# The first batch of an attention and mixer kernel as one explicit order of steps, with four MLP accumulations begun among the last mixer pieces

## The chip, the cores and the metric

The kernel runs on one core of one Trainium2 chip. The metric is the device time of one execution in microseconds (us). TensorE (PE) multiplies and writes PSUM; VectorE (DVE), ScalarE (ACT) and GpSimd (POOL) do the rest; SyncE (SP) and POOL issue DMAs. Each engine executes its own instructions in the order of the program and waits for others through semaphores.

## The reference

Eight sequences of 448 tokens, 12 heads of 64. Attention with normalised queries and keys, then a mixer that adds a low-rank mix over the tokens, then an MLP of 768 to 3072 to 768:

```python
q_n, k_n = rmsnorm(q, g_q), rmsnorm(k, g_k)
attn = softmax(q_n @ k_n.T / sqrt(64))
x = (attn @ v) with the heads side by side        # 8 x 448 x 768
h = x.transpose(0, 2, 1) @ U @ V                  # rank 32, over the tokens
u = x + h.transpose(0, 2, 1)
out = u + relu(u @ w_ch1) @ w_ch2
```

## The kernel before, in words

Heads are taken in groups of four (24 groups, three to a batch), and in pairs of heads (six to a batch). For a group, q and k are loaded (`load`, SP), squared (`squares`), summed (`sums`, DVE), turned into 1/rms (`roots`, two small ACT steps), scaled (`scale`, mostly POOL), transposed on PE (`turn`) and copied out of PSUM (`take_q`, `take_k`). `values` (POOL) casts v. For a pair, `Sc` multiplies keys and queries in four steps r = 0 to 3 (the first three write 128x896, the last 128x448) and ACT takes the exponential of each; `V` multiplies the exponentials with the values in two halves, and DVE divides by the sums into `x`.

For batch 0, `mix_t0` multiplies x with U, and `mix(dt)` makes one of six 128-row pieces of `uT`, the mixer's output, turned. An MLP accumulation `up(b, ht)` is six matmuls over the six pieces `dt` of `uT` with one of 24 column blocks of w1, then a relu; `down` multiplies with w2. w1 comes in four quarters and w2 in eight parts, cast on the way, all issued by POOL through `weights(n)`; the first quarter of w1 serves the accumulations 0 to 5.

The program order is fixed by hand (`tc.manual_schedule()`): what is called first stands first in the queue of its engine. Batch 0's attention is alone on the chip: the rows of `extra` say what is put behind which `Sc`, with `keep_busy` (dummy matmuls) where PE would stand still. Two MLP accumulations of batch 0 are begun early with `up_part` in one half of a score buffer each: three matmuls, one, and the last two in the MLP's list. From `first_done` on, a planner merges two lists: `att`, the attention of the next batches, and `mlp`, with estimated costs; `due(cm)` says how far attention should be, and `ready` holds a step back while ACT or DVE are behind PE. Group 3 belongs to batch 1; its squares and sums lie in the front, its scaling and turning at the head of the second part of `att`.

Score buffers (`ps_sc`) are two, of two PSUM banks each; all else in PSUM shares four buffers of one bank (`ps`).

Of the kernel before, what the change touches and what calls it, by code (L numbers as in the profile page):

```python
# [26 lines left out]
def kernel(  # L27
# [19 lines left out]
    P = 128  # L47
# [199 lines left out]
    for va, vl in zip(va_bufs, vl_bufs):  # L247
        nc.vector.memset(va[:, :, D:D1], 1.0)
        nc.vector.memset(vl, 0.0)
        for e in range(2):  # L250
            nc.vector.memset(vl[e * R:(e + 1) * R, :, e * D1 + D:(e + 1) * D1], 1.0)
# [9 lines left out]
    def prep_gains():  # L261
        m = gp[:, P:]
        nc.vector.tensor_reduce(m, gp[:, :D], AX, ALU.max, apply_absolute_value=True)
        nc.vector.tensor_scalar(m, m, -scal * D, EXP_ROOM, ALU.mult, ALU.add)
        nc.vector.tensor_scalar(m, m, 0.0, -EXP_SHIFT, ALU.min, ALU.max)
# [3 lines left out]
        return pg  # L269
# [42 lines left out]
    nc.gpsimd.memset(Vr[:, S:], 0.0)  # L312
# [15 lines left out]
    def fill_mixer():  # L328
        nc.gpsimd.memset(Uz, 0.0)

# [13 lines left out]
    def turn(gi, i):  # L344

        pt = pts[(gi, i)] = ps.tile([P, NT, 2, R], BF16, name="pt", tag="ps")
        pos = POS_ODD if i == 0 and groups[gi][0] % 2 else POS
        for j in range(NT):
            nc.tensor.transpose(pt[:, pos[j]].rearrange("p a r -> p (a r)"),  # L349
                                normed[gi][i][:, j].rearrange("p c d -> p (c d)"), ident)  # L350

    def take_q(gi, a, scalar=False):
# [6 lines left out]
        qk[(gi, a)] = [qT]  # L359

    def take_k(gi, a):
# [6 lines left out]
        qk[(gi, a)].append(kT)  # L368
# [29 lines left out]
    def Sc(b, pr, r):  # L398
# [9 lines left out]
        for i in range(n):  # L408
            d = slice(i * D, (i + 1) * D) if r < NJ else slice(0, P)
            nc.tensor.matmul(sc[:, i, :S], kT[d, keys], qT[d], start=True, stop=True)  # L410
        nc.scalar.activation(es[(b, pr)][:, 2 * r:2 * r + n, :], sc[:, :n, :S], AF.Exp, scale=scal, bias=bias)  # L411
        runs("pe", 0.25)
# [32 lines left out]
    def V(b, pr, half):  # L445
        at["pe"] = max(at["pe"], exp_done[(b, pr)])
# [5 lines left out]
        h0 = groups[gi][1] + first_h  # L452
        E = es[(b, pr)]
        pv = ps.tile([P, 2, 2, D1], FP32, name="pv", tag="ps")
        for i in range(2):
# [3 lines left out]
            for e in range(2):  # L459
                for j in range(NJ):  # L460
                    nc.tensor.matmul(pv[:, i, e, :], E[:, 2 * j + e, w:w + P],  # L461
                                     va[:, (first_h + step * e) * NJ + j, :], start=False, stop=(e == 1 and j == NJ - 1))
        r = headp.tile([P, 2, 2], FP32, name="r", tag="r")
# [4 lines left out]
            r.rearrange("p i e -> p i e ()").to_broadcast([P, 2, 2, D]), ALU.mult)  # L468
        runs("pe", 0.5)
        runs("dve", 0.6)  # L470

# [38 lines left out]
    def mix_t0(lo, hi, scalar=False):  # L510

        pt = ps.tile([P, 512], FP32, name="pu0", tag="ps")
        for j in range(NW):
            nc.tensor.matmul(pt[:, :hi - lo], Uz[:, j, :], xs[0][:, j, lo:hi], start=(j == 0), stop=(j == NW - 1))
        if scalar:
            nc.scalar.copy(tz[:, lo:hi], pt[:, :hi - lo])
        else:
            nc.vector.tensor_copy(tz[:, lo:hi], pt[:, :hi - lo])

    def mix(b, dt, scalar=False):  # L520
        off = 64 if b % 2 == 0 else 0
        ph = ps.tile([P, S], FP32, name="ph", tag="ps")
        xb = xs[b][:, :, dt * P:(dt + 1) * P]
# [4 lines left out]
        if scalar:  # L528
            nc.scalar.copy(uT[:, dt, off:off + S], ph)
        else:  # L530
            nc.vector.tensor_copy(uT[:, dt, off:off + S], ph)
# [36 lines left out]
    begun = {}  # L568

    def up_part(b, ht, lo, hi):  # L570
        off = 64 if b % 2 == 0 else 0
        if lo == 0:
            begun[(b, ht)] = ps_sc.tile([P, 2, 512], FP32, name="sc", tag="sc")[:, 0, :S]
        ph = begun[(b, ht)]
        for dt in range(lo, hi):
            nc.tensor.matmul(ph, w1b[:, dt, ht * P:(ht + 1) * P], uT[:, dt, off:off + S],
                             start=(dt == 0), stop=(dt == KD - 1))
        if hi == KD:
            nc.scalar.activation(hT[:, ht, off:off + S], ph, AF.Relu)
# [60 lines left out]
    def V2(i, half):  # L640
        return (0.55, V, (*pairs[i], half))

    pool = nc.gpsimd

    def scales(gi):
        return [(0, roots, (gi,)), (0, scale, (gi, 0, pool)), (0, scale, (gi, 1, pool))]

    def turns(gi):
        return [(0.4, turn, (gi, 0)), (0, take_q, (gi, 0)), (0, take_q, (gi, 1)), (0.4, turn, (gi, 1)), (0, take_k, (gi, 0))]

    extra = {
        (0, 0): [(0, keep_busy, (8,))],
        (0, 1): [(0, keep_busy, (8,))],
        (0, 2): scales(1) + [(0, squares, (2, 1, pool)), (0, keep_busy, (8,))],
        (0, 3): [(0, keep_busy, (8,))],
        (1, 0): [(0, keep_busy, (8,))],
        (1, 1): [V2(0, 0), (0, keep_busy, (6,))],
        (1, 2): [(0.4, turn, (1, 0)), (0, take_q, (1, 0)), (0, take_q, (1, 1)), (0, keep_busy, (8,))],
        (1, 3): [(0.4, turn, (1, 1)), (0, take_k, (1, 0)), V2(0, 1), (0, take_k, (1, 1)), (0, sums, (2, 1)),
                 (0, values, (1,)), (0, load, (4,)), (0, weights, (1,))],  # L660
        (2, 1): scales(2) + [(0, weights, (1,)), V2(1, 0)],
        (2, 2): [(0, keep_busy, (6,))],
        (2, 3): [V2(1, 1), (0, prep_u, ())],
        (3, 0): [(0, keep_busy, (6,))],
        (3, 1): [V2(2, 0)],
        (3, 2): turns(2),
        (3, 3): [V2(2, 1), (0, take_k, (2, 1)), (0, squares, (3, 0, pool)), (0, values, (2,)), (0, load, (5,)),
                 (0, weights, (1,)), (0, prep_v, ()), (0, squares, (3, 1, pool)), (0, weights, (1,))],
        (4, 0): [V2(3, 0)],
        (4, 1): [V2(3, 1), (0, sums, (3, 0))],  # L670
        (5, 0): [(0.9, mix_t0, (0, 512))],
        (5, 1): [V2(4, 0)],
        (5, 2): [V2(4, 1), (0.39, mix, (0, 0))],
        (5, 3): [(0.39, mix, (0, 1)), (0.2, mix_t0, (512, 640)), (0, weights, (2,))],
    }
    for i in range(NPAIR):
        for r in range(4):
            add_att(0.38, Sc, *pairs[i], r)
            att.extend(extra.get((i, r), []))
    att.extend([V2(5, 0), V2(5, 1), (0, sums, (3, 1)), (0.39, mix, (0, 2, True)), (0.39, mix, (0, 3, True)), (0.57, up_part, (0, 0, 0, 3)),  # L680
                (0.2, mix_t0, (640, dm)), (0.39, mix, (0, 4, True)), (0, roots, (3,)), (0.57, up_part, (0, 1, 0, 3)),
                (0.39, mix, (0, 5)), (0.19, up_part, (0, 0, 3, 4)), (0.19, up_part, (0, 1, 3, 4))])
    first_done = len(att)

    att.extend([*scales(3)[1:2], (0, scale, (3, 1, nc.vector)), (0, values, (3,)), (1.4, lambda: None, ()),
# [78 lines left out]
    done_at = {}  # L764
    for n, (c, f, a) in enumerate(att):
        if f is V and a[1] == NPAIR - 1 and a[2] == 1:
            done_at[a[0]] = n + 1 if a[0] > 0 else first_done
# [4 lines left out]
    for b in range(B):  # L772
        for ht in range(KH):
            mlp.append((0.38, up_part, (b, ht, 4, KD), b) if b == 0 and ht < 2 else (1.14, up, (b, ht), b))
            if b < ROWS_FROM and ht % 2 == 0 and ht < 4 * NW:
                mlp.append((0.17, mix_rows, (b, ht // 4, ht // 2 % 2), b))
# [21 lines left out]
    a_, b_ = PARTS  # L798
    squares_part(0, *a_)
    squares_part(0, *b_)  # L800
    sums_part(0, *a_)
    sums_part(0, *b_)
    squares_part(1, *a_)
    roots(0, 0, 1)
    squares_part(1, *b_)
    for part in PARTS:
        scale_part(0, *part, nc.gpsimd)
    for part in PARTS:
        sums_part(1, *part)
    roots(0, 1, 2)  # L810
    pg = prep_gains()
    keep_busy(10)
    for part in PARTS:
        scale_part(1, *part, nc.vector)
    nc.vector.tensor_copy(gg, pg)
    squares(1, 0)
    fill_mixer()
    squares(2, 0, nc.gpsimd,
            uT.rearrange("p k c -> p (k c)")[:, :4 * NT * D].bitcast(FP32).rearrange("p (j d) -> p j d", d=D))
    values(0)  # L820
    turn(0, 0)
    keep_busy(14)
    take_q(0, 0, True)
    take_q(0, 1, True)
    squares(1, 1)
    turn(0, 1)
    take_k(0, 0)
    sums(1, 0)
    sums(1, 1)
    take_k(0, 1)  # L830
    sums(2, 0)
    stage_tiles(3)
    load_u()
    load_v(2)
    load_qk(3, 0)
    load_qk(3, 1)
    load_v(3)

    ia = im = 0
# [109 lines left out]
```

## Time and profile before

| what | value |
|---|---|
| three runs | 577.03, 578.73, 578.82 us (median 578.73) |
| profiled execution | 577.21 us, span 575.3 us |
| granted TensorE clock | 0.999 |
| PE, ACT, POOL, DVE busy | 98%, 53%, 36%, 34% |
| DMA, mean | 119 GB/s over the span |
| first exponential starts | 11.61 us |
| last exponential of batch 0 ends | 35.10 us |
| last piece of `uT` of batch 0 is copied | 39.97 us |

The profile is of one execution; its times count from the start of the span, and the execution took 1.9 us more than the span. The first rows are of whole executions; the last three are rows of the timeline and say where the stage ends that the change is about.

### The profile page before, as it was taken

What the parts mean: (1) busy time and instruction counts of PE and PEld (TensorE: products, weight loads), DVE (VectorE), ACT (ScalarE), POOL (GpSimd) and SP (SyncE); (2) the same over time, 40 slices, a digit from 0 to 9 for tenths busy, and PEclk for the clock granted to TensorE, in tenths of its full rate; (3) what the DMA queues carried; (4) which work ended last, traced back from release to release, by engine and by line L of the source; (5) the groups of instructions that cost most, each with busy time, mean ns of one, the idle gap of its engine ahead of it and who ended that gap; (6) DMA issues with size and microseconds to landing.
All of it is one profiled execution on the core that took longest, in us unless ns stands there. A gap on an engine that the chain in (4) does not pass through costs nothing.

```text
span 575.3 us, 11525 instructions
## 1 busy us (share of the span) xinstructions
PE 565.6 (98%) x4723; PEld 326.0 (57%) x4724; DVE 194.2 (34%) x452; ACT 307.3 (53%) x510; POOL 205.3 (36%) x302
## 2 busy tenths in 40 slices
PE   8899999999999999999999999999999999999997
PEld 7655555555655555555556555555565555555565
DVE  6676655412343221631335330443033310410011
ACT  6867661677453876367654578367762444014300
POOL 4884683365423615324524423442531000000000
PEclk9999999999999999999999999999999999999999
DMA  9899999875436842597245835276204210320022
GB/s 244 161 242 241 245 230 216 147 166 118 126 66 168 176 115 35 97 212 180 33 128 106 188 100 131 58 184 152 35 14 97 57 28 1 61 70 1 1 55 56
DMA packets 104828, 68.19 MB, mean 119 GB/s; under 512 B 66632, under 2 KB 101704, under 8 KB 104776
## 3 DMA queue, kind: packets, MB, share of 16 engines
q1 hardware_dynamic: 95124, 57.83, 44.6%
q0 software_dynamic: 9408, 9.44, 9.8%
q8 instruction: 37, 0.61, 0.5%
q10 hardware_dynamic: 244, 0.20, 0.1%
q14 instruction: 15, 0.12, 0.1%
HBM read 52.20 MB, written 11.01 MB: 110 GB/s over the span
## 4 chain that ended last, share of the span: by engine, by line
PE 93%; DMA 2%; ACT 2%; POOL 1%; issue 1%; DVE 1%; SPq 0%; POOLq 0%; ACTq 0%
PE ph L558 38%; PE po L605 36%; PE pv L461 6%; PE sc L431 2%; PE pv L457 2%; PE sl L422 2%; PE sl L433 2%; PE po L592 1%; DMA qf<-in_q_dram 1%; PE sc L410 1%; DMA vf<-in_v_dram 1%; ACT E L411 1%; PE sc L496 1%; PE pt L349 1%; POOL kp L174 1%
## 5 line engine op out<-in xcount | busy, mean ns | idle before, releaser
L558 PE MATMUL ph<-uT,w1b 128*128 128x448 bf16 x1140 | 228.8, 352 | 0.0
L605 PE MATMUL po<-w2b,hT 128*128 128x384 bf16 x1296 | 223.8, 326 | 0.0
L605 PEld LDWEIGHTS <-hT 128*128 128x128 bf16 x1296 | 123.0, 98 | 79.0 <-issue 2.5
L558 PEld LDWEIGHTS <-w1b 128*128 128x128 bf16 x1140 | 108.2, 98 | 93.9 <-issue 1.1
L565 ACT ACTIVATE hT<-ph 128x448 bf16<-128x448 f32 x184 | 98.0, 553 | 118.7 <-PE ph L558 117.2
L381 POOL TENSOR_SCALAR qT<-qT,gg 128x448 bf16<-128x448 bf16 x36 | 50.4, 1403 | 87.4 <-DMA qT<-qn 79.6
L424 ACT ACTIVATE E<-sl,gg 128x448 bf16<-128x448 f32 x72 | 41.7, 634 | 69.8 <-PE sl L422 69.8
L464 DVE RECIPROCAL r<-pv 128x4 f32<-128x4 f32 x96 | 17.4, 181 | 167.4 <-PE pv L461 167.1
L193 POOL TENSOR_TENSOR qn<-qf,rs 128x384 bf16<-128x384 f32 x36 | 29.9, 830 | 120.8 <-ACT rs L170 114.6
L436 ACT ACTIVATE E<-sc,gg 128x896 bf16<-128x896 f32 x72 | 69.2, 1028 | 0.0
L615 DVE TENSOR_TENSOR ob<-po,x 128x384 f32<-128x384 f32 x46 | 25.6, 557 | 113.7 <-PE po L605 109.7
L461 PE MATMUL pv<-va,E 128*128 128x65 bf16 x1152 | 57.1, 194 | 0.0
L461 PEld LDWEIGHTS <-E 128*128 128x128 bf16 x1152 | 50.5, 98 | 6.2
L162 DVE TENSOR_REDUCE ssq<-sq 128x14 f32<-128x896 f32 x45 | 46.8, 1079 | 3.1 <-ACT sq L140 2.6
L457 PE MATMUL pv<-vl,E 128*128 128x130 bf16 x192 | 42.3, 220 | 0.3 <-ACT E L411 0.2
L465 DVE TENSOR_TENSOR x<-pv,r 128x256 bf16<-128x256 f32 x96 | 40.7, 424 | 3.3
L411 ACT ACTIVATE E<-sc,gg 128x896 bf16<-128x896 f32 (+1 forms) x42 | 37.5, 952 | 3.5 <-PE sc L410 3.4
L193 POOL TENSOR_TENSOR kp<-kf,rs 128x384 bf16<-128x384 f32 x36 | 29.8, 829 | 0.0
L503 DVE TENSOR_TENSOR x<-sc,x 128x384 bf16<-128x384 f32 x42 | 20.8, 551 | 15.7 <-PE sc L496 15.7
L169 ACT ACTIVATE rs<-ssq,eps 128x28 f32<-128x28 f32 (+1 forms) x25 | 7.9, 314 | 34.0 <-DVE ssq L162 31.3
L457 PEld LDWEIGHTS <-E 128*128 128x128 bf16 x192 | 18.7, 97 | 10.4 <-issue 2.7
L434 ACT ACTIVATE E<-sl,gg 128x448 bf16<-128x448 f32 x36 | 23.1, 642 | 0.0
(103 smaller groups left out, 364.5 us busy)
## 6 DMA issues: line engine op xcount, KB each, us to landing
qf<-in_q_dram SPq DMA_DIRECT2D x23, 448.0 KB, 3.9
kf<-in_k_dram SPq DMA_DIRECT2D x23, 448.0 KB, 5.0
vf<-in_v_dram SPq DMA_DIRECT2D x48, 192.0 KB, 5.6
out_dram<-ob SPq DMA_DIRECT2D x48, 192.0 KB, 2.7
w1b<-in_moe_w_ch_dram POOLq DMA_DIRECT2D x4, 1152.0 KB, 20.3
w2b<-in_moe_w_ch_dram POOLq DMA_DIRECT2D x8, 576.0 KB, 18.8
vf<-in_v_dram SPq DMA_DIRECT2D x48, 32.0 KB, 5.1
out_dram<-ob SPq DMA_DIRECT2D x13, 96.0 KB, 3.8
```

The lines of the kernel that those rows point to most:

```text
L162: nc.vector.tensor_reduce(ssqs[gi][:, i, :], sqs.pop((gi, i)), AX, ALU.add)
L193: nc.gpsimd.tensor_tensor(main.rearrange("p (t i) d -> p i t d", i=2), src[:, c, :2 * NJ].rearrange("p (i t) d -> p i t d", i=2), rs[:, c, ...
L381: nc.gpsimd.tensor_scalar(qT[:, a], qT[:, a], gg[:, 0:1], None, ALU.mult)
L411: nc.scalar.activation(es[(b, pr)][:, 2 * r:2 * r + n, :], sc[:, :n, :S], AF.Exp, scale=scal, bias=bias)
L424: nc.scalar.activation(E[:, 4 + i, :], ts[i], AF.Exp, scale=scal, bias=bias)
L436: nc.scalar.activation(E[:, 2 * r:2 * r + 2, :], tiles[r][:, :, :S], AF.Exp, scale=scal, bias=bias)
L457: nc.tensor.matmul(pv[:, i].rearrange("p e d -> p (e d)"), E[:, 2 * NJ, w:w + P], vl[:, lp, :], start=True, stop=False)
L461: nc.tensor.matmul(pv[:, i, e, :], E[:, 2 * j + e, w:w + P], va[:, (first_h + step * e) * NJ + j, :], start=False, stop=(e == 1 and j == N ...
L465: nc.vector.tensor_tensor(xs[b].rearrange("p i (h d) -> p i h d", d=D)[:, 2 * half:2 * half + 2, h0:h0 + step + 1:step, :], pv[:, :, :, :D ...
L558: nc.tensor.matmul(ph, w1b[:, dt, ht * P:(ht + 1) * P], uT[:, dt, off:off + S], start=(dt == 0), stop=(dt == KD - 1))
L565: nc.scalar.activation(hT[:, ht, off:off + S], ph, AF.Relu)
L605: nc.tensor.matmul(po, hT[:, ht, col:col + P], w2b[:, ht, half * HALF:(half + 1) * HALF], start=(ht == 0), stop=(ht == KH - 1))
```

## The change

Batch 0 is no longer given by `extra` and a prelude of calls, but by one string, `FRONT`, of steps in the order in which they are called. A step is `name.arguments:engine`. So every step of every engine has a place of its own: `S` and `E` are the two halves of `Sc` (matmuls, exponential), `V` and `N` those of `V` (matmuls, normalisation), `mt` and `mtc` those of `mix_t0` (now in four chunks of 256, 256, 128 and 128 columns instead of 512, 128 and 128), `mix` and `mc` those of `mix`. `sqp`, `smp`, `rt0`, `scp` are the parts of group 0; `sq`, `sm`, `rt`, `sc`, `tq`, `tk` are squares, sums, roots, scaling, `take_q`, `take_k`; `b` is `keep_busy`, `w` issues one quarter of w1, `u.ht.dt` is one matmul of an MLP accumulation. `:a`, `:v`, `:p` are ACT, DVE, POOL.

- Four MLP accumulations instead of two are begun, in the four banks of the two score buffers, and all 24 of their matmuls, with the relus, stand in the front. The MLP's list starts at accumulation 4.
- Squares: those of group 2's keys go from POOL to ACT; those of group 1's keys go ahead of those of its queries and ahead of `take_q` of group 0; group 0's go second part first. Group 3's stand behind the front on POOL.
- Sums, roots and scaling of group 3 go to the planner's part.
- Some fills go from DVE to POOL or back, two small steps on the gains from DVE to POOL, and their maximum ahead of group 0's sums.
- The quarters of w1 are issued at other places: the first behind `val.1`, where POOL no longer has the square of group 2's keys ahead of it.
- Group 0's turn has its pieces in another order, dummy matmuls go from 90 to 66 (without the 72 at the start), and `ready` lets a `Spair` go with ACT at most 0.6 behind PE, not 1.0.

```diff
-    for t, eng in zip(kT_bufs, (nc.vector, nc.gpsimd)):
-        eng.memset(t[D:P, :, SM:S], 0.0)
-        eng.memset(t[0:D, :, S:], 0.0)
+    for i in range(2):
+        fill_values(i, nc.vector)
+    fill_keys(0, nc.vector)
...
     def fill_mixer():
         nc.gpsimd.memset(Uz, 0.0)
+        fill_values(2, nc.gpsimd)
+        fill_keys(1, nc.gpsimd)
...
-    def up_part(b, ht, lo, hi):
...
+    AHEAD = 4
+    begun, dts = [], {}
+
+    def up_one(ht, dt):
+        if ht // 2 == len(begun):
+            begun.append(ps_sc.tile([P, 2, 512], FP32, name="sc", tag="sc"))
+        ph = begun[ht // 2][:, ht % 2, :S]
+        n = dts[ht] = dts.get(ht, 0) + 1
+        nc.tensor.matmul(ph, w1b[:, dt, ht * P:(ht + 1) * P], uT[:, dt, 64:64 + S], start=(n == 1), stop=(n == KD))
+        if n == KD:
+            nc.scalar.activation(hT[:, ht, 64:64 + S], ph, AF.Relu)
...
-    extra = {
...
-        (0, 2): scales(1) + [(0, squares, (2, 1, pool)), (0, keep_busy, (8,))],
...
-        (3, 3): [V2(2, 1), (0, take_k, (2, 1)), (0, squares, (3, 0, pool)), (0, values, (2,)), (0, load, (5,)),
-                 (0, weights, (1,)), (0, prep_v, ()), (0, squares, (3, 1, pool)), (0, weights, (1,))],
...
-    att.extend([*scales(3)[1:2], (0, scale, (3, 1, nc.vector)), (0, values, (3,)), (1.4, lambda: None, ()),
+    att.extend([(0, sums, (3, 0)), (0, sums, (3, 1)), (1.0, lambda: None, ()), (0, roots, (3,)), (0, scale, (3, 0, pool)),
+                (0, scale, (3, 1, nc.vector)), (0, values, (3,)), (1.4, lambda: None, ()),
                 (0.4, turn, (3, 0)), (0.4, turn, (3, 1)), (0, take_q, (3, 0)), (0, take_q, (3, 1)),
...
-        for ht in range(KH):
-            mlp.append((0.38, up_part, (b, ht, 4, KD), b) if b == 0 and ht < 2 else (1.14, up, (b, ht), b))
+        for ht in range(AHEAD if b == 0 else 0, KH):
+            mlp.append((1.14, up, (b, ht), b))
...
+    FRONT = """
+        sqp.0.1:a sqp.0.0:a gr smp.0.1 gains sqp.1.0:a smp.0.0 pg sqp.1.1:a smp.1.0 rt0.0 smp.1.1 scp.0.1:p gg rt0.1 scp.0.0:p
+        scp.1.1:v sq.1.1:a scp.1.0:v turn.0.0 sq.1.0:a b.6 turn.0.1 b.14 tq.0.0:a tk.0.0 sq.2.0:p tq.0.1:a sm.1.0 S.0.0 S.0.1
+        E.0.0 b.10 sm.1.1 E.0.1 S.0.2 val.0 b.6 sm.2.0 rt.1 S.0.3 b.14 E.0.2 tk.0.1 sc.1.0 E.0.3 S.1.0 sq.2.1:a S.1.1 sc.1.1
+        turn.1.0 E.1.0 V.0.0 tq.1.0:v V.0.1 sm.2.1 E.1.1 S.1.2 val.1 turn.1.1 tq.1.1:v E.1.2 S.1.3 tk.1.0 b.10 E.1.3 w N.0.0
+        S.2.0 rt.2 S.2.1 tk.1.1 E.2.0 V.1.1 prepu N.0.1 V.1.0 sc.2.1 E.2.1 N.1.1 S.2.2 b.6 E.2.2 S.2.3 sc.2.0 turn.2.1 E.2.3
+        S.3.0 tk.2.1 E.3.0 S.3.1 tk.2.0 V.2.1 prepv E.3.1 turn.2.0 N.1.0 S.3.2 N.2.1 V.2.0 E.3.2 w tq.2.0:v S.3.3 mt.0 N.2.0
+        E.3.3 w S.4.0 tq.2.1:v E.4.0 S.4.1 mtc.0 V.3.0 w E.4.1 mix.0 N.3.0 S.4.2 val.2 V.3.1 E.4.2 S.4.3 mix.1 N.3.1 E.4.3 S.5.0
+        mc.0:v mt.1 E.5.0 S.5.1 mtc.1 V.4.0 E.5.1 mc.1:v S.5.2 N.4.0 mix.3 E.5.2 S.5.3 V.4.1 E.5.3 mix.2 u.0.0 mc.3:a u.1.0
+        mc.2:v u.0.1 V.5.0 N.4.1 V.5.1 N.5.0 mt.2 u.1.1 N.5.1 u.2.0 u.2.1 u.3.0 mtc.2 u.3.1 u.0.3 mt.3 u.1.3 u.2.3 mtc.3 u.3.3
+        mix.4 mix.5 mc.4:v u.0.2 u.1.2 mc.5:a u.2.2 u.3.2 u.0.4 u.1.4 u.2.4 u.3.4 u.0.5 u.1.5 u.2.5 u.3.5
+    """
...
+        "gains": lambda eng: prep_gains(pool),
...
+        "w": lambda eng: weights(1),
+        "S": lambda pr, r, eng: scores(0, pr, r),
+        "E": lambda pr, r, eng: exps(0, pr, r),
...
     load_u()
     load_v(2)
-    load_qk(3, 0)
-    load_qk(3, 1)
-    load_v(3)
-
+    for step in FRONT.split():
+        step, _, eng = step.partition(":")
+        name, *a = step.split(".")
+        steps[name](*map(int, a), engines[eng])
+        if step == "scp.0.0":
+            fill_mixer()
+        if name == "val":
+            load(int(a[0]) + 3)
+    for i in range(2):
+        squares(3, i, pool)
+    weights(2)
+
+    at.update(pe=0.0, act=0.0, dve=0.0)
...
-            return at["dve"] <= at["pe"] + 0.3 and at["act"] <= at["pe"] + 1.0
+            return at["dve"] <= at["pe"] + 0.3 and at["act"] <= at["pe"] + 0.6
```

More of the change, by code (lines that the diff above doesn't have):

```diff
@@ L347, in turn @@
         pos = POS_ODD if i == 0 and groups[gi][0] % 2 else POS
-        for j in range(NT):
+        for j in (*range(*PARTS[1]), *range(*PARTS[0])) if gi == 0 else range(NT):
             nc.tensor.transpose(pt[:, pos[j]].rearrange("p a r -> p (a r)"),
@@ L462, in V, with norms @@
                                      va[:, (first_h + step * e) * NJ + j, :], start=False, stop=(e == 1 and j == NJ - 1))
+    def norms(b, pr, half):
+        gi, lp = divmod(b * NPAIR + pr, 2)
+        first_h, step = (2 * lp, 1) if gi == BESIDE else (lp, 2)
+        h0 = groups[gi][1] + first_h
+        pv = pvs.pop((b, pr, half))
         r = headp.tile([P, 2, 2], FP32, name="r", tag="r")
@@ L508, in mix_two, with mix_t0, keep_t0, mix @@
             nc.sync.dma_start_transpose(uT[:, :, c:c + hi - lo], full)
-    def mix_t0(lo, hi, scalar=False):
-        pt = ps.tile([P, 512], FP32, name="pu0", tag="ps")
+    CHUNKS = ((0, 2 * P), (2 * P, 4 * P), (4 * P, 5 * P), (5 * P, dm))
+    pus, phs = {}, {}
+    def mix_t0(c):
+        lo, hi = CHUNKS[c]
+        pt = pus[c] = ps.tile([P, 512], FP32, name="pu0", tag="ps")
         for j in range(NW):
             nc.tensor.matmul(pt[:, :hi - lo], Uz[:, j, :], xs[0][:, j, lo:hi], start=(j == 0), stop=(j == NW - 1))
[L515 to L523, printed above, removed]
+    def keep_t0(c):
+        lo, hi = CHUNKS[c]
+        nc.vector.tensor_copy(tz[:, lo:hi], pus.pop(c)[:, :hi - lo])
+    def mix(dt):
+        ph = phs[dt] = ps.tile([P, S], FP32, name="ph", tag="ps")
+        xb = xs[0][:, :, dt * P:(dt + 1) * P]
         nc.tensor.matmul(ph, tz[:, dt * P:(dt + 1) * P], Vr[:, :S], start=True, stop=False)
@@ L566, in up @@
             runs("act", 0.45)
-    begun = {}
-    def up_part(b, ht, lo, hi):
[L571 to L579, printed above, removed]
+    AHEAD = 4
[8 more added lines that the diff above has]
+            nc.scalar.activation(hT[:, ht, 64:64 + S], ph, AF.Relu)
     down_ps, down_sb = {}, {}
@@ L676 @@
[L676 to L682, printed above, removed]
@@ new lines, with square_of @@
+    """
+    engines = {"a": nc.scalar, "v": nc.vector, "p": pool, "": None}
+    beside = uT.rearrange("p k c -> p (k c)")[:, :4 * NT * D].bitcast(FP32).rearrange("p (j d) -> p j d", d=D)
+    def square_of(gi, i, eng):
+        eng = None if eng is nc.scalar else eng
+        squares(gi, i, eng, beside if (gi, i) == (2, 0) else None)
+    steps = {
+        "sqp": lambda i, p, eng: squares_part(i, *PARTS[p], None if eng is nc.scalar else eng),
+        "smp": lambda i, p, eng: sums_part(i, *PARTS[p]),
+        "rt0": lambda i, eng: roots(0, i, i + 1),
+        "scp": lambda i, p, eng: scale_part(i, *PARTS[p], eng),
+        "gr": lambda eng: most_gain(),
+        "gains": lambda eng: prep_gains(pool),
+        "pg": lambda eng: spread_gains(),
+        "gg": lambda eng: nc.vector.tensor_copy(gg, pgs[0]),
+        "turn": lambda gi, i, eng: turn(gi, i),
+        "tq": lambda gi, a, eng: take_q(gi, a, eng is nc.scalar),
+        "tk": lambda gi, a, eng: take_k(gi, a),
+        "sq": square_of,
+        "sm": lambda gi, i, eng: sums(gi, i),
+        "rt": lambda gi, eng: roots(gi),
+        "sc": lambda gi, i, eng: scale(gi, i, pool),
+        "val": lambda gi, eng: values(gi),
+        "w": lambda eng: weights(1),
+        "S": lambda pr, r, eng: scores(0, pr, r),
+        "E": lambda pr, r, eng: exps(0, pr, r),
+        "V": lambda pr, half, eng: products(0, pr, half),
+        "N": lambda pr, half, eng: norms(0, pr, half),
+        "b": lambda n, eng: keep_busy(n),
+        "mt": lambda c, eng: mix_t0(c),
+        "mtc": lambda c, eng: keep_t0(c),
+        "mix": lambda dt, eng: mix(dt),
+        "mc": keep_u,
+        "u": lambda ht, dt, eng: up_one(ht, dt),
+        "prepu": lambda eng: prep_u(),
+        "prepv": lambda eng: prep_v(),
+    }
```

140 lines of the change are left out of this document (49 added, 91 removed).

## The prediction

> **What bounds the kernel now.** I read the page first, then the busy time by stretches, the chain of waits, the timelines of ACT and POOL in the first 40 us, and last the DMA issues one by one.
>
> ```profile
> span 575.3 us, 11525 instructions
> ...
> PE 565.6 (98%) x4723; PEld 326.0 (57%) x4724; DVE 194.2 (34%) x452; ACT 307.3 (53%) x510; POOL 205.3 (36%) x302
> ```
>
> TensorE is the limit, but 98% is a mean over stages. By stretches:
>
> ```profile
> 11.00:35.00 24.00, 21.19 (x293) 14.46 (x294) 17.52 (x50) 21.70 (x29) 21.27 (x24) 1.00 0.97 189
> 40.00:100.00 60.00, 59.76 (x529) 33.32 (x528) 35.62 (x81) 32.62 (x52) 36.67 (x41) 1.00 1.21 233
> 100.00:560.00 460.00, 459.54 (x3639) 258.54 (x3632) 129.23 (x282) 244.36 (x412) 139.94 (x220) 1.00 0.44 98
> ```
>
> The columns are the stretch, its length, then PE, PEld, DVE, ACT, POOL busy. From 40 us on PE has no gap worth the name: PE's waits after 40 us sum to 0.7 us. So the rest of the program is a fixed amount of PE work, and the change is worth what it moves that work forward. From 11 to 35 us ACT is the full engine (21.70 of 24.00), although much of PE's 21.19 there are dummy matmuls. The seam between the two shows in the chain of waits:
>
> ```profile
> 39.34 0.64 DVE uT L531
> 39.97 0.04 issue
> 40.01 0.35 PE sc L576
> ```
>
> At 40.01 the last piece of `uT` is there and PE runs on without a stop. Eight MLP matmuls (2 accumulations x 4 pieces) are done by then. ACT's timeline gives the pace before it:
>
> ```profile
> 10.77 0.95 ACT L140 ACTIVATE sq<-kf 128x896 f32<-128x896 f32 x1
> 11.61 2.81 ACT L411 ACTIVATE E<-sc,gg 128x896 bf16<-128x896 f32 x3
> ...
> 19.88 1.91 ACT L411 ACTIVATE E<-sc,gg 128x896 bf16<-128x896 f32 x2 [1.03 <-PE sc L410]
> 22.04 0.32 ACT L169 ACTIVATE rs<-ssq,eps 128x28 f32<-128x28 f32 x1 [0.25 <-DVE ssq L162]
> ...
> 34.47 0.63 ACT L411 ACTIVATE E<-sc,gg 128x448 bf16<-128x448 f32 x1 [0.25 <-PE sc L410]
> ```
>
> The exponentials run from 11.61 to 35.10. Three wide ones in 2.81 us are 0.90 from start to start; a narrow one takes 0.53, so a pair costs 3 x 0.90 + 0.53 = 3.23. The idle times in brackets (2.1 us in all) can be filled.
>
> **The yardstick.** The front of the changed kernel ends with 24 MLP matmuls done, 16 more than before. One costs 0.19 (six in 1.14 on the chain). The old kernel would stand there at 40.01 + 16 x 0.19 = 43.05. The gain is 43.05 less the time T at which the new front ends.
>
> **Start of the exponentials.** ACT now takes both squares of group 1 ahead of `take_q`, the key's first (`sq.1.1`). The keys of group 1 are the issue at 2.26:
>
> ```profile
> kf<-in_k_dram SPq DMA_DIRECT2D x1, 448.0 KB, 7.2
> ```
>
> They land at 9.46. Before, that square ran at 10.77, behind both `take_q`, and did not wait. Now ACT waits until 9.5, squares (0.84 to the next start, twice), takes q (0.53 twice), and the first exponential starts at 9.5 + 1.68 + 1.06 = 12.3, 0.7 later than before. DVE's added 0.2 us reduction for the gains and POOL's two scalings of one value (not in the trace; between DVE's 0.14 and POOL's 0.31 each, I take 0.31, the same engine) move the scaling of group 0 by about 0.5 us. It is hidden: keys turned by 11.1, queries not before 11.8. The fills moved to POOL (about 1 us, from rows of 0.1 to 0.2 each) go into its 2.20 us of idle time before 11.20; without that cover they would cost their 1 us.
>
> **ACT up to the last exponential.** From 12.3: two wide ones, roots (0.50), a wide and a narrow one, the square of group 2's keys (0.84, moved from POOL), pair 1 (3.23), roots (0.50): pair 2 starts at 20.6, against 19.88. But the second roots, which cost 0.73 with their wait at 22.04, are done. Four pairs at 3.23 end at 33.6; before it was 35.10. DVE has some 10.4 us of work in those 13 us, POOL's scaled group 2 is ready by 24.4, needed by 26, and values of group 2 by 29.6, needed at 31; I cost these waits at nothing, up to 0.5.
>
> **TensorE's tail, if nothing else holds it.** `u.0.0` can start at about 33.4, when the score buffer of `S.5.2` is free. From there PE has: 3 MLP matmuls 0.57, two halves of V at 0.50, `mt.2` 0.22, 6 matmuls 1.14, `mt.3` 0.22, 3 matmuls 0.57, two `mix` at 0.39, 12 matmuls 2.28: 6.78. The chain behind the last exponential (values, normalisation 0.6, `mt.3`, copy 0.3, `mix.5`, copy 0.53) is some 4.9 and hides in it: before, PE waited in that chain. T would be 40.2, a gain of 2.9.
>
> **The weights.** This is where I expect most of it to stop. All matmuls behind `u.0.0` queue on PE, V of the last pair too, and `u.0.0` reads the first quarter of w1. POOL's timeline and the DMA issues between 21.2 and 22.5 us:
>
> ```profile
> 18.30 1.68 POOL L143 TENSOR_TENSOR sq<-kf 128x896 f32<-128x896 f32 x1
> 19.93 0.82 POOL L201 CAST va<-vf 128x768 bf16<-128x768 f32 x1
> 20.69 0.64 POOL L203 CAST vl<-vf 64x128 bf16<-64x128 f32 x2
> 21.27 1.05 POOL L278 DMA_DIRECT2D w1b<-in_moe_w_ch_dram  x1
> ```
> ```profile
> w1b<-in_moe_w_ch_dram POOLq DMA_DIRECT2D x1, 1152.0 KB, 15.5
> ```
>
> Before, it lands at 21.27 + 15.5 = 36.8, and the first MLP matmul starts at 36.93: no slack. After, POOL loses the square in front of it (1.63 from start to start), and its first scaling of group 1 starts 0.2 earlier, since the roots do. The issue is at 19.4, the landing at 34.9. PE stands from 33.4 to 34.9, and T = 34.9 + 6.78 = 41.7: a gain of 1.35.
> The Trainium skill (DMA: Bandwidth & Descriptors, Anatomy of one DMA) fits a POOL-issued transfer as 2.0 us plus bytes over 436 GB/s; by that estimate the quarter would take 4.7 us, land at 24.1 and T would be 40.2. The trace disagrees (15.5, with the queues at a share of 1.05 or more), so the sum goes by 15.5.
> The second quarter lands 8.7 behind the first before (26.04 + 19.4 = 45.4), so at 43.6 after; its first reader, accumulation 6, comes at T + 2.4 = 44.1. Just covered. POOL then issues the other three quarters at about 25.5 to 28 (before 26.04, 31.60, 35.25) and, after group 3's squares, the first two parts of w2 at 33 (before 36.13); they queue behind the first quarter, so they cost it nothing. `prep_u` and `prep_v`, moved behind the issues, are read at 26 or later. SP's loads keep their order, and SP is paced by the DMA, not by the steps.
>
> **Behind the front.** Sums, roots and scaling of group 3 now follow the front instead of lying in it. DVE's sums (2.1) lie beside the last matmuls. Roots come two accumulations later; DVE scales in 2.22 beside POOL's 1.68, until about T + 5.6, and PE wants to turn at T + 4.9 to 5.5. I take a wait of 0.3 (0 to 0.6). The stricter gate for `Spair` (0.6 instead of 1.0) reorders a stage in which PE already has no gaps; I take nothing, at most 0.7 either way, PE's waits there.
>
> **Sum.** 1.35 - 0.3 = 1.05 us. The profiled execution took 577.21 (span 575.3 and 1.9 around it), so 576.2 on its scale; the median of the three runs is 578.73, 1.5 above, which gives 577.7.
>
> **The rivals.**
> A, the forecast, weights set T: 0.50. Its ends are a landing at 34.3 and no wait in the turn (gain 1.95), and a landing at 35.8 (gain 0.2).
> B, the weights arrive in time: 0.22. The 15.5 contains 3.7 us between the end of the issue (22.3) and the first packets of POOL's queue (26.1 in the DMA view), which may shrink. Then T = 40.2, gain 2.9 less 0.3: 576.1. For it: POOL's issue falls nearer the thin stretch of DMA at 16 to 20 us (75 GB/s). Against it: all twelve weight transfers took 13 us or more.
> C, the early accumulations bring nothing, since the landing does not follow the issue: 0.12. If the loads ahead in the queues set it, it stays at 36.8, T = 43.6, 0.5 lost, and 0.3 in the turn: 579.5.
> D, slower: 0.16. The issue hangs on a row of POOL steps (two scalings, one copy of values) behind ACT's roots, and these behind the wait for the keys at 9.46. Where DVE and POOL scaled together at 39.9, DVE took 2.22 and POOL's next copy 1.67 instead of 0.82. Doubling POOL's three steps would add up to 4.7 us; half of that, or a key 2.5 us late, puts the landing at 37.3 and T at 44.1. With the turn's wait, any landing past 36.0 loses time and past 37.7 it loses over 1.7. I price it at 38.2: 2.2 lost, 580.9.
> In D PE would stand for over 3.4 us; the Trainium skill (TensorE: Matmul & The Clock Gate, The HAM clock gate) says that an idle window of that length halves the clock, which would add up to 1.7. The first 72 dummies, 5.37 us of weight loads for 72 against 0.56 for 10 later, agree with a cold start.
>
> **Numbers.** About 0.3%, 1.7 us, is what a measurement here can tell. Faster by more: B 0.22 and the upper end of A 0.14, 0.36. Same: 0.36 of A and 0.10 of C, 0.46. Slower: D 0.16 and 0.02 of C, 0.18. The range runs from B with its unknowns, 575.3, to the near side of D, 580.4; A alone spans 576.8 to 578.5.
>
> **What would show it.** Right: first exponential at 12.3, last one ending near 33.6, PE idle before the first matmul on w1 and that wait ended by the DMA, landing near 35, the last of 24 matmuls near 41.7, no PE gaps after. Wrong: `u.0.0` without a wait (B), the landing at 36.8 (C), a late issue on POOL (D), or PE gaps beyond 45 us, which I do not expect.

## The result and the profile after

The changed kernel is slower: 579.71 us (median) against 577.45 us, a ratio of 1.0038 (95% interval 1.0022 to 1.0054). The forecast was 577.7, and a gain or no change was held more likely than this loss of 2.3 us.

One execution of the changed kernel took 1167.96 us, with TensorE at about half its rate from the first instruction to the last (its MLP matmuls took 622 ns in the mean instead of 353, and its trace holds no entry of the clock, so the granted clock of 1.000 in its profile says nothing); its cause stays open, and it is left out of all comparisons. The profile read here is another one, a0, of 581.12 us (span 579.2), which is 1.4 above the median. Its page and its busy time by the same stretches:

```profile
span 579.2 us, 11482 instructions
...
PE 564.7 (97%) x4704; PEld 324.8 (56%) x4704; DVE 192.9 (33%) x449; ACT 307.1 (53%) x510; POOL 204.4 (35%) x306
```

```profile
11.00:35.00 24.00, 20.49 (x285) 13.66 (x284) 15.62 (x46) 23.89 (x34) 21.67 (x26) 1.00 0.93 186
40.00:100.00 60.00, 56.27 (x500) 31.49 (x498) 34.68 (x80) 33.72 (x55) 34.84 (x38) 1.00 1.21 226
100.00:560.00 460.00, 460.00 (x3650) 258.34 (x3649) 131.07 (x287) 244.50 (x412) 142.33 (x223) 1.00 0.43 98
```

From 11 to 35 us ACT is now full (23.89 of 24.00, 21.70 before). But from 40 to 100 us PE, which had lost 0.24 us of 60 before, now loses 3.73. From 100 us on it loses nothing (0.46 before). So the time went between 35 and 100 us. The waits of PE from 20 us to the end name the places:

```profile
PE sc L619 <- DMA w1b<-in_moe_w_ch_dram: 1.8, 1, 1.8
PE sc L619 <- ACT hT L621: 1.5, 2, 0.9
PE pt L368 <- POOL qn L178: 1.3, 1, 1.3
```

The columns are total, times, longest. The first wait was forecast. The second was not, and the third was put at 0.3. PE's timeline shows where each one falls:

```profile
36.75 0.74 PE L619 MATMUL sc<-uT,w1b 128*128 128x448 bf16 x3 [1.80 <-DMA w1b<-in_moe_w_ch_dram]
...
41.24 1.87 PE L619 MATMUL sc<-uT,w1b 128*128 128x448 bf16 x9
43.74 0.54 PE L619 MATMUL sc<-uT,w1b 128*128 128x448 bf16 x2 [0.63 <-ACT hT L621]
45.15 0.35 PE L619 MATMUL sc<-uT,w1b 128*128 128x448 bf16 x1 [0.88 <-ACT hT L621]
45.34 1.30 PE L601 MATMUL ph<-uT,w1b 128*128 128x448 bf16 x6
...
51.70 0.51 PE L368 MATMUL pt<-ident,qn 128*128 128x128 bf16 x6 [1.34 <-POOL qn L178]
```

The front ends at T = 45.34, not at 41.7, and 2.3 us behind the yardstick of 43.05. The gaps of PE after T sum to 3.06 us, against 1.02 after that point before. (They are counted from the start of one matmul to that of the next, less the usual spacing; the brackets count from a matmul's modelled end and are some 0.17 shorter.) Together that is 4.3 us; the two spans differ by 3.9, so 0.4 of it stays unexplained.

Ahead of that, ACT's timeline (two stretches) and POOL's show how the start moved:

```profile
10.84 0.95 ACT L140 ACTIVATE sq<-kf 128x896 f32<-128x896 f32 x1 [3.09 <-DMA kf<-in_k_dram]
11.69 0.93 ACT L140 ACTIVATE sq<-qf 128x896 f32<-128x896 f32 x1
12.53 1.14 ACT L375 ACTIVATE qT<-pt,gg 128x448 bf16<-128x448 bf16 x2
13.60 1.90 ACT L435 ACTIVATE E<-sc,gg 128x896 bf16<-128x896 f32 x2
...
32.66 2.42 ACT L435 ACTIVATE E<-sc,gg 128x896 bf16<-128x896 f32 x3
```

```profile
17.75 1.69 POOL L178 TENSOR_TENSOR kp<-kf,rs 128x896 bf16<-128x896 f32 x1
19.38 0.83 POOL L205 CAST va<-vf 128x768 bf16<-128x768 f32 x1
20.15 0.64 POOL L207 CAST vl<-vf 64x128 bf16<-64x128 f32 x2
20.73 1.07 POOL L295 DMA_DIRECT2D w1b<-in_moe_w_ch_dram  x1
```

```profile
w1b<-in_moe_w_ch_dram POOLq DMA_DIRECT2D x1, 1152.0 KB, 16.0
```

The keys of group 1 are there at 10.81 us instead of 9.46, although their load is issued where it was. ACT stands 3.09 us for them, and the first exponential starts at 13.60, not 12.3. The weights are issued at 20.73 instead of 19.4 and land 16.0 later, at 36.71.

### The profile page after: what moved, and what is told of

It reads as the page before. It is cut to its first block, busy times and chain, and to the rows that moved or that the text cites. A ratio compares the mean times of both kernels' runs of the same rounds, so it can differ in the third digit from the quotient of the medians.

```text
span 1166.1 us, 11482 instructions
## 1 busy us (share of the span) xinstructions
PE 1159.6 (99%) x4704; PEld 508.4 (44%) x4704; DVE 194.4 (17%) x449; ACT 317.8 (27%) x510; POOL 204.7 (18%) x306
## 4 chain that ended last, share of the span: by engine, by line
PE 99%; ACT 0%; DVE 0%; POOL 0%; issue 0%; POOLq 0%
PE ph L601 40%; PE po L647 39%; PE pv L490 6%; PE sc L460 3%; PE pv L486 2%; PE sc L430 1%; PE po L634 1%; PE busy L244 1%; PE sl L462 1%; PE sl L451 1%; PE pt L368 1%; PE sc L619 1%; PE pu L519 0%; PE sc L535 0%; PE pu L556 0%; PE pm L589 0%
## 5 line engine op out<-in xcount | busy, mean ns | idle before, releaser
L601 PE MATMUL ph<-uT,w1b 128*128 128x448 bf16 x1128 | 476.1, 622 | 0.0
L647 PE MATMUL po<-w2b,hT 128*128 128x384 bf16 x1296 | 468.3, 564 | 0.0
L647 PEld LDWEIGHTS <-hT 128*128 128x128 bf16 x1296 | 186.8, 147 | 232.9 <-issue 229.6
L601 PEld LDWEIGHTS <-w1b 128*128 128x128 bf16 x1128 | 161.2, 146 | 263.7 <-issue 262.8
L490 PE MATMUL pv<-va,E 128*128 128x65 bf16 x1152 | 100.4, 255 | 0.0
L453 ACT ACTIVATE E<-sl,gg 128x448 bf16<-128x448 f32 x72 | 41.7, 632 | 214.3 <-PE sl L451 214.3
L490 PEld LDWEIGHTS <-E 128*128 128x128 bf16 x1152 | 90.9, 132 | 20.9 <-issue 19.7
L486 PE MATMUL pv<-vl,E 128*128 128x130 bf16 x192 | 60.6, 315 | 0.0
L460 PE MATMUL sc<-qT,kT 64*128 64x448 bf16 x144 | 37.3, 619 | 0.0
L486 PEld LDWEIGHTS <-E 128*128 128x128 bf16 x192 | 26.2, 136 | 22.6 <-issue 22.6
```

Of the source, the lines that this page charges most:

```text
L453: nc.scalar.activation(E[:, 4 + i, :], ts[i], AF.Exp, scale=scal, bias=bias)
L460: nc.tensor.matmul(tiles[r][:, i, :S], kT[d, r * P:(r + 1) * P], qT[d], start=True, stop=True)
L486: nc.tensor.matmul(pv[:, i].rearrange("p e d -> p (e d)"), E[:, 2 * NJ, w:w + P], vl[:, lp, :], start=True, stop=False)
L490: nc.tensor.matmul(pv[:, i, e, :], E[:, 2 * j + e, w:w + P], va[:, (first_h + step * e) * NJ + j, :], start=False, stop=(e == 1 and j == N ...
L647: nc.tensor.matmul(po, hT[:, ht, col:col + P], w2b[:, ht, half * HALF:(half + 1) * HALF], start=(ht == 0), stop=(ht == KH - 1))
```

## The experiments

In the profiles of the experiments, "keys" is the landing of group 1's keys, "issue" and "landing" are those of the first quarter of w1, T is the first MLP matmul behind the 24 early ones, and "gaps" are PE's gaps over 0.2 us after T. Each row has one profile and one median, which are not of the same execution. Medians are given with the ratio to the kernel before and its 95% interval; one interval is about 0.6 us to each side (0.9 for the changed kernel), so a difference of two medians of 1 us, as for p1, p6 and p7 below, is at the edge of what can be told. The waits and times inside the profiles are firmer.

| kernel | median, ratio [interval] | keys | issue, landing | T | gaps |
|---|---|---|---|---|---|
| p4, kernel before again | 577.63, 1.0007 [0.9995, 1.0019] | 10.18 | 21.72, 37.08 | | 1.26 |
| a0, changed again | 581.12, one run | 10.81 | 20.73, 36.71 | 45.34 | 3.06 |
| p1 | 578.72, 1.0019 [1.0009, 1.0029] | 8.93 | 18.85, 34.05 | 40.85 | 3.93 |
| p2 | 583.63, 1.0103 [1.0090, 1.0116] | 9.50 | 10.22, 23.36 | 48.29 | 3.05 |
| p3 | 580.55, 1.0049 [1.0035, 1.0063] | 9.67 | 19.59, 35.35 | 43.98 | 3.67 |
| p5 | 579.72, 1.0037 [1.0022, 1.0051] | 10.71 | 20.64, 36.13 | 44.76 | 3.05 |
| p6 | 578.59, 1.0017 [1.0002, 1.0032] | 8.96 | 18.87, 34.73 | 43.37 | 2.49 |
| p7 | 578.90, 1.0025 [1.0014, 1.0036] | 10.85 | 19.42, 33.94 | 43.42 | 3.06 |
| c3 | 578.03, 1.0013 [1.0002, 1.0024] | 10.94 | 19.33, 34.29 | 41.48 | 4.95 |
| c6 | 578.48, 1.0015 [1.0004, 1.0026] | 11.35 | 21.30, 36.62 | 43.41 | 2.81 |
| c4 | 577.98, 1.0002 [0.9992, 1.0013] | 10.27 | 18.74, 33.74 | 40.91 | 4.16 |
| c5 | 576.07, 0.9978 [0.9969, 0.9988] | 9.68 | 18.13, 33.07 | 40.27 | 2.96 |

**a0 and p4: each kernel profiled once more, unaltered.**

> The changed kernel unaltered, for a profile at the usual matmul rate (the profiled execution on record ran all of its matmuls at about half rate: 622 ns instead of 352). Theory L (the wait for the first quarter of w1 has grown past the point where it loses time): PE stands still before the first u matmul for 3 us or more, ended by the landing of the first quarter at 37 us or later, and nearly all of the 2.2 us lost stands at the last of the 24 u matmuls (about 45.0 instead of the old kernel's 43.05). Rival S (the loss is behind the front): the 24 matmuls end at 42 to 43 us, and PE has new gaps, 2 to 3 us in all, after 45 us.

> The old kernel for a second profile. In its first profile the keys of group 1 landed at 9.46, in two of the changed kernel at 10.81 and 11.9. Theory V: the landing varies from execution to execution, and a late one costs the old kernel nothing (its square of these keys stands behind take_q and starts at 10.8 anyway); here too it may land at 10 to 12, with the first exponential still at 11.6 to 12. Rival: the change delays it; then it lands at 9.5 again.

a0 has something of both theories: T stands where the first put it, with a wait of 1.80 and not 3 or more, and PE has 2.0 us of new gaps behind it.

The kernel before does not wait for these keys: at 10.18 instead of 9.46 their square still starts later (11.21). Its span is 575.8 instead of 575.3 because its whole start, from the first load on (landed at 4.65 instead of 4.20), is 0.4 later. In the changed kernel's order the keys landed between 8.93 and 11.35 in eleven profiled executions, and at 11.90 in that of 1167.96 us, with nothing altered in the loads ahead of them. So the landing is a quantity that varies from one execution to the next. Whether the changed kernel also makes it later on the whole, two executions against twelve cannot say.

**p1: one relu for both banks of a score buffer.**

```diff
-        if n == KD:
-            nc.scalar.activation(hT[:, ht, 64:64 + S], ph, AF.Relu)
+        if n == KD and ht % 2:
+            nc.scalar.activation(hT[:, ht - 1:ht + 1, 64:64 + S], begun[ht // 2][:, :, :S], AF.Relu)
```

> The relus of the four early accumulations two by two (one 128x896 step after the second accumulation of a buffer instead of a narrow one after each). Theory R: u.1.5 and u.3.5 write a buffer that ACT still reads, and wait 0.8 and 1.0 us for the narrow relu; without it PE runs the 12 last matmuls without a gap, the 24th ends 1.8 us earlier after its weights, and the time falls by about 1.8 us, to 577.9 or so against 579.7. Rival: the wait only hides others that follow (DVE's sums, roots, the turn of group 3); then the gaps go but PE stands as much longer before the turn, and the time stays within 0.5 us.

The waits on L621 are gone, and T follows `u.0.0` by 6.76 us, where it was 8.59 in a0. 6.78 was forecast. The same holds in every profile: 8.58 to 8.59 in the six with one relu for each bank, 6.75 to 6.76 in the five with one for both. The median is 1.0 lower, less than the 1.84 that PE stood there, and the profile shows what gives some of it back, a wait at 109.8 us that a0 does not have:

```profile
PE pt L368 <- POOL qn L178: 1.3, 1, 1.3
PE sc L430 <- ACT E L435: 0.7, 4, 0.2
PE ph L601 <- DMA uT<-u_rest: 0.7, 1, 0.7
PE sc L619 <- DMA w1b<-in_moe_w_ch_dram: 0.5, 1, 0.5
```

**p2: the first quarter of w1 issued at 10.2 us**, ahead of the square of group 2's queries.

```diff
-    ... tq.0.0:a tk.0.0 sq.2.0:p ...  E.1.3 w N.0.0
+    ... tq.0.0:a tk.0.0 w sq.2.0:p ...  E.1.3 N.0.0
```

> The first quarter of w1 is issued about 10 us earlier, ahead of the square of group 2's queries on POOL, while the queues still carry the first loads. Theory W: u.0.0 then does not wait (1.80 us before), and the time falls by up to 1.8 us, to about 577.9, if the group loads behind it are not needed earlier than they come. Rival: the early transfer takes the queues from the loads of groups 1 and 2 (turn about, packet by packet), these land 2 us or more later, the exponentials shift by as much, and the time stays or rises to 580 to 582.

It lands at 23.36, PE's wait for it is gone, and the kernel is 4 us slower. POOL's timeline shows the loads that now come later:

```profile
10.22 1.07 POOL L295 DMA_DIRECT2D w1b<-in_moe_w_ch_dram  x1
...
16.43 1.69 POOL L178 TENSOR_TENSOR kp<-kf,rs 128x896 bf16<-128x896 f32 x1
19.90 0.82 POOL L205 CAST va<-vf 128x768 bf16<-128x768 f32 x1 [1.78 <-DMA vf<-in_v_dram]
```

POOL now waits 5.1 us for values and U between 8 and 40 us (0.2 in a0, where it waits 2.5 for queries instead), ACT stands 4.5 us in one gap, and the last exponential ends at 40.0 instead of 35.1. Issued at 20 us the same 1152 KB leave no such waits; issued at 10 us they come with several. A second loss follows from them: PE stands 4.11 us for the scaled keys of group 2, and the granted clock is 0.50 from 25.8 to 32.7 us and 1.00 on either side. This is the halving that the prediction put into rival D. How the 4 us divide between late loads and clock was not tried.

**p3: the gate of `Spair` back at 1.0.**

```diff
-            return at["dve"] <= at["pe"] + 0.3 and at["act"] <= at["pe"] + 0.6
+            return at["dve"] <= at["pe"] + 0.3 and at["act"] <= at["pe"] + 1.0
```

> Only the gate of Spair goes back to 1.0. Theory: the steady stage has no PE gaps under either value, so the time stays at 579.7 within 0.5 us. Rival G: the stricter gate is part of the loss; then the time falls by 1 us or more.

No gain: the median is 0.8 higher, more than the 0.5 that was allowed, but the ratio's interval overlaps that of the changed kernel.

**p5: the key's square of group 1 back behind the query's and `take_q`.**

```diff
-        scp.1.1:v sq.1.1:a scp.1.0:v turn.0.0 sq.1.0:a b.6 ... tq.0.1:a sm.1.0
+        scp.1.1:v sq.1.0:a scp.1.0:v turn.0.0 b.6 ... tq.0.1:a sq.1.1:a sm.1.0
```

> The square of group 1's keys goes back behind both take_q, that of its queries stays ahead. Theory K (ACT's wait for keys that land between 8.9 and 11.9 sets the first exponential, and through the roots POOL's issue of w1): the first exponential starts at 11.5 to 12.1 whatever the landing, the first issue of w1 comes at 19.0 to 19.6, and the time falls by 0.5 to 1.5 us from 579.7, with less spread. Rival: the roots of group 1 wait for the moved square and its sum instead; then the issue of w1 does not move and the time stays.

ACT no longer stands for the keys, which were late again (10.71):

```profile
10.74 0.95 ACT L140 ACTIVATE sq<-kf 128x896 f32<-128x896 f32 x1 [0.26 <-DMA kf<-in_k_dram]
11.59 1.89 ACT L435 ACTIVATE E<-sc,gg 128x896 bf16<-128x896 f32 x2
13.37 0.31 ACT L173 ACTIVATE rs<-ssq,eps 128x28 f32<-128x28 f32 x1
```

The first exponential is 2.0 us earlier than in a0, and so are the roots of group 1 (13.37, against 15.39). The issue of w1 is only 0.1 earlier. What holds it is the row of POOL steps ahead of it, which starts with the square of group 2's queries, here in a0 and in p5:

```profile
12.69 1.68 POOL L143 TENSOR_TENSOR uT<-qf 128x896 f32<-128x896 f32 x1 [2.49 <-DMA qf<-in_q_dram]
```

```profile
12.63 1.68 POOL L143 TENSOR_TENSOR uT<-qf 128x896 f32<-128x896 f32 x1 [2.36 <-DMA qf<-in_q_dram]
16.01 1.69 POOL L178 TENSOR_TENSOR qn<-qf,rs 128x896 bf16<-128x896 f32 x1
```

These queries are the load behind the keys of group 1, landed at 12.53 and 12.47 (11.06 in the kernel before). POOL is free for the scaling of group 1 at 16.00 in a0 and at 15.93 in p5. The roots end at 15.97 in a0, at the same time, and at 13.94 in p5, where they then win nothing. So the rival was right that the issue does not move, but not in its reason. While the weights set T, an earlier exponential is worth next to nothing.

**p6: the roots of group 3 ahead of the planner's cost item.**

```diff
-    (0, sums, (3, 1)), (1.0, lambda: None, ()), (0, roots, (3,)), ... (1.4, lambda: None, ()),
+    (0, sums, (3, 1)), (0, roots, (3,)), ... (2.4, lambda: None, ()),
```

> The empty cost of 1.0 ahead of group 3's roots is moved behind them, so that roots and scaling are issued before the MLP goes on while the turn keeps its place. Theory T: PE's wait of 1.5 us before the turn of group 3 goes (scaling ends 2 us earlier), and the time falls by 1.2 to 1.5 us, to about 578.3. Rival: the wait passes on to the copies behind the turn or to the score buffers, and the time stays within 0.5 us.

The wait at L368 is gone and the median 1.1 lower; a wait of 0.77 for `u_rest` at 110.8 us takes part of it, as in p1.

**p7: the first quarter of w1 ahead of the copy of group 1's values.**

```diff
-    ... S.1.2 val.1 turn.1.1 ... E.1.3 w N.0.0
+    ... S.1.2 w val.1 turn.1.1 ... E.1.3 N.0.0
```

> POOL issues the first quarter of w1 ahead of the values of group 1 instead of behind them: 1.35 us earlier, and still behind the loads of groups 0 to 2. Theory L: the landing follows the issue (15 to 16 us behind it), the wait of u.0.0 shrinks from 1.6 to 1.8 us to some 0.4, and the time falls by 1.2 us, to about 578.5. Rival: the landing is set by the loads ahead in the queues; then it stays where it was relative to them and the time does not fall.

The issue is 1.31 earlier than in a0 at equally late keys, the landing 2.77, PE's wait for w1 is gone and the median is 0.8 lower. The landing follows the issue, here by 14.5 us.

**c3: p1, p5, p6 and p7 together.**

> All four mends: paired relus, the squares' order, the roots ahead, the first quarter of w1 ahead of group 1's values. If the four waits are separate, their gains add up to 4.5 to 5.5 us: 574.5 to 575.5, 0.3 to 0.5% under the old kernel's 577.4. If they cover one another, it stays at 576.5 or above.

The front now beats the yardstick by 1.57 us even with keys at 10.94, and the time is still above that of before. PE's timeline and waits say where it went:

```profile
99.32 2.11 PE L647 MATMUL po<-w2b,hT 128*128 128x384 bf16 x12 [1.96 <-DMA w2b<-in_moe_w_ch_dram]
```

```profile
PE po L647 <- DMA w2b<-in_moe_w_ch_dram: 2.0, 1, 2.0
PE ph L601 <- DMA uT<-u_rest: 1.1, 1, 1.1
```

The last of w2's eight parts lands at 99.28 us and PE asks for it at 97.36. In the kernel before it landed at 97.17 and PE read it at 97.73, so there were 0.6 us to spare. PE is thus only 0.4 earlier here, though the front leads by 1.57; the part is 2.1 later, and it was issued 1.7 later (80.75, against 79.09). From 60 to 100 us the DMA share is 1.21 or more in either kernel, so the queues had no room to make up for it. 1.96 + 1.10 us are waited there, twice the lead of the front.

**c6: p1 and p6 alone.**

> The changed kernel with only two edits: one relu over both banks of a score buffer (p1) and group 3's roots ahead of the cost item (p6). Theory: the whole loss of 2.3 us against before is these two waits, which the prediction missed or under-sized; alone they brought 1.0 and 1.1 us, so together 577.6, equal to before within 0.3%, with no PE wait on ACT's relu after 20 us and none over 0.3 us in the turn of group 3. Rival: the two are not additive, because an earlier batch 1 runs into the transfers of w2 and of batch 1's mixer, as in c3; then PE waits 1 us or more between 90 and 112 us, and the time is 578.4 to 578.8, that of p1 or p6 alone.

The rival fits better, though narrowly: 577.6 would be a ratio of 1.0002, just outside the interval. The two gains do not add up in the median (578.48; p1 and p6 alone 578.72 and 578.59). The two waits aimed at are gone, and the profile shows what is left:

```profile
PE sc L619 <- DMA w1b<-in_moe_w_ch_dram: 1.1, 1, 1.1
PE ph L601 <- DMA uT<-u_rest: 1.1, 1, 1.1
```

The transpose of `u_rest` stands on SP's queue behind output stores and the transposes of `x`; there it is issued at 109.45 us, and PE asks for it at 110.88. In the kernel before it was issued at 107.60 and PE read it at 110.12, without a wait; in p4 (108.03) PE already waited 0.08, so there was nothing to spare. PE is 0.8 later in c6 than before, and the issue 1.9. In a0 it was issued at 110.82, and PE came only at 114.15. Why SP moves up less than PE was not tried.

This profile also shows a lower clock, which no list of waits names. ACT's late start (the keys landed at 11.35) left PE standing 2.40 us before 13.74, and the granted clock was 0.50 from 13.96 to 17.38 us.

**c4 and c5: c3 with w2's parts asked for sooner, then with the turn sooner.**

```diff
-                weights(2)
+                weights(4 if a[0] == 4 else 2)
```
```diff
-    ... (2.4, lambda: None, ()),
+    ... (1.4, lambda: None, ()),
```

> The kernel with all four mends, and four parts of w2 instead of two issued behind group 4's scaling (the last two then behind group 5's). In the kernel without this the front ended 1.6 us ahead of the old one, and PE then stood 2.1 us at 97 us until the last part of w2 had landed (99.3), and 1.3 us at 111 us for the turned rest of the mixer. Theory D (the gain of the front is given back at the weights of w2, since the queues are full up to 100 us): with the parts issued 5 to 12 us earlier the wait at 97 us goes and the time falls by 1.5 to 2 us, to 576.2 or so, under the old kernel's 577.4. Rival: the queues are full in any order; then a load or a transpose comes late instead, and the time stays at 578.

> As the kernel with four parts of w2 together, and group 3's turn 1.0 of planned cost earlier (the empty cost behind its roots back to 1.4), so that batch 1's attention starts about 2 us sooner. If its late start is what leaves the short PE gaps at 50 to 82 us (0.4, 0.6, 0.3, 0.3), they shrink and the time falls by a further 0.5 to 1 us; if the turn then waits for the scaling again, it rises by up to 1.3.

In c4 the last part lands at 97.9 and the wait for it falls from 2.0 to 1.2; the median is that of c3 within its interval. In c5, which plans the turn of group 3 1.0 us sooner, the last part lands at 96.0 and these are all the waits of PE after 20 us:

```profile
PE pt L368 <- POOL qn L178: 1.0, 1, 1.0
PE sc L430 <- ACT E L435: 0.4, 2, 0.2
PE sc L430 <- DVE kT L383: 0.3, 1, 0.3
PE pt L368 <- POOL kp L178: 0.3, 1, 0.3
PE ph L601 <- DMA uT<-u_rest: 0.2, 1, 0.2
PE ph L601 <- ACT E L435: 0.2, 1, 0.2
```

A wait of 1.0 in the turn is back, the waits for w2 and nearly all of that for `u_rest` (issued at 106.46, 1.1 earlier than in the kernel before) are gone, and 576.07 us beats both kernels: 0.22% below before (interval 0.12 to 0.31%). The trace shows that the transfers come earlier with the sooner turn; that this alone is the cause was not tried by itself, and c5's keys also landed 0.6 earlier than c4's.

## Why the prediction was wrong, step by step

The miss can be added up on the profile. T was forecast at 41.7 and came at 45.34, 3.64 later, and the wait in the turn was 1.2 longer than forecast. That is 4.84; 576.2 on the profile's scale plus 4.84 is 581.0, and the execution took 581.12. (PE's smaller gaps after T sum to 0.5 more than before, which this leaves out, so the agreement is closer than the sum deserves.)

- **"The first exponential starts at 12.3": mis-sized by 1.3, through its first term.** The steps behind the keys cost what was said (2.76 from the start of the square to the exponential). "They land at 9.46" was read off one execution of the kernel before and taken as fixed. It is the earlier of that kernel's two, and 1.35 earlier than here. The kernel before did not show it, because its square came later anyway. (9.5 + 1.68 + 1.06 is 12.24, rounded up.)
- **"The issue is at 19.4, the landing at 34.9": mis-sized, again by landings taken as fixed.** The issue came 1.3 later and the landing took 16.0 instead of 15.5: 1.81 of the 3.64. The prediction hung the issue on the roots, and these on the keys. POOL's own row hangs as much on the queries of group 2, 1.47 later here than before, and p5 shows that earlier roots alone do not move it. Rival D had the row, hung on the keys alone and priced at keys 2.5 us late; 1.35 came. Its other half, POOL steps slowed by DVE, did not happen: the scalings before the issue took their 1.69.
- **"From there PE has 6.78": the step that failed.** All the listed work was right (36.75 + 6.78 = 43.53), and two waits were missing: the other 1.84. `u.0.5` ends an accumulation in one bank of a score buffer, its relu reads that bank, and `u.1.5`, next on PE, writes the other bank of the same buffer. PE waits for the relu, as it does again at `u.3.5`: 0.80 and 1.04 between matmuls, of which the profile's brackets show 0.63 and 0.88. Before, the two early accumulations had a buffer each. The diff shows both (`begun[ht // 2]`), and the prediction counted only matmuls. p1 shows it: with one relu for both banks the tail is 6.76. Late keys alone do not explain the loss: in p3 and p6, whose fronts are the same as a0's, earlier keys (9.67 and 8.96) still give T = 43.98 and 43.37, behind the yardstick of 43.05; without the 1.84 both would be ahead of it.
- **"I take a wait of 0.3 (0 to 0.6)": mis-sized, 1.5.** PE wanted the turn at T + 5.0, as forecast. The scaling was done at T + 6.3 instead of 5.6: roots at T + 3.1, and POOL's scaling beside DVE's took 2.59, where 1.68 was assumed for POOL and 2.22 for DVE. This time POOL was the slow one, having begun 0.05 behind DVE; before, DVE had begun 0.41 behind POOL. p6 takes the wait out.
- **"Four pairs end at 33.6": right in its length**, shifted by the late start: the last one ends at 35.08.
- **The gate at nothing: right** as far as p3 can tell. **Rival C, a landing that does not follow the issue: refuted** (p2, p7); that its 579.5 lies close to the measured 579.71 is luck. **Rival B:** p2 shows weights in time and a loss of 4 us; in p7 they are in time too, and the relus still hold T at 43.42. **Rival D's halved clock:** PE's longest wait in a0 after 20 us was 1.80, and its clock held; p2, with a wait of 4.11, shows the halving. The estimate from the Trainium skill (DMA: Bandwidth & Descriptors, Anatomy of one DMA), 4.7 us for a quarter of w1, was not approached by any profiled execution; 13.1 us, in p2, was the shortest for the first quarter.
- **The offset of 1.5 to the median was an artefact of three runs.** With eight runs the median of before is 577.45, 0.2 above the profiled execution; on that scale the forecast was 576.4. So the miss is 3.3 us, and that 577.7 lies only 2.0 off is luck.
- **"From 40 us on the rest is a fixed amount of PE work": only as far as before went.** The kernel before had 0.6 us to spare at the last part of w2 and nothing at `u_rest`, and "no gap" hides both. In c3 and c4, with fronts 1.6 and 2.1 us ahead, both transfers came later than before and took the lead back; in c5 they came earlier, and cost next to nothing. Had the front gained its 1.35, part would probably have been lost there; that was not tried by itself.

What stays open: the late keys cannot be told from chance with these runs, and c6 leaves 1.0 us of the loss (interval 0.2 to 1.5), for which its waits for w1 and for `u_rest`, its late keys (11.35) and the halved clock behind them are what the profile offers. The clock is a cost that the prediction did not have outside D. In 26 of 100 executions of the changed kernel and its variants (without p2 and that of 1167.96 us) the mean granted clock is 0.997 or less, and they took 1.0 us more than the others of the same kernel in the mean; of 99 of the kernel before, one did so. That the late keys bring it about is argued from c6's profile alone. Why w2 and `u_rest` come later in c3 and c4 than before was not tried.

## What to carry to other kernels

When accumulations share a PSUM buffer, look for the reader of one half that stands between the writers of the two; a sum of matmul times does not contain that wait. A step moved ahead of a load's landing turns the landing's scatter into time, so take landings from several executions, not one. Before crediting a stage with its whole lead, ask which transfers the next stages need at the earlier time and how long before their use they landed so far; a wait of nothing can mean that there was nothing to spare.

## What was not expected of the hardware

- The same load, issued at the same place, landed between 8.93 and 11.90 us in twelve profiled executions.
- When DVE and POOL scaled at once, the one that began second took longer: before, POOL began at 39.47 (1.68) and DVE at 39.88 (2.22); in a0 DVE began at 49.01 (1.09) and POOL at 49.06 (2.59). p4 repeats the first pair, and all ten variants the second.
- PE stood 4.11 us in p2 and 2.40 us in c6, and the granted clock was then 0.50 for 6.8 and for 3.4 us. In a0 PE stood 2.19 us at the same place as in c6, and the clock held.
